# Attention with two mixture layers on one core: nine stores on ScalarE's queue, a reordered end of the first stage, and a later start of one attention pair

## The chip, the core and the metric

The kernel runs on one core of a Trainium2 chip. The metric is the device time in microseconds (us) of one execution; of several runs the median is taken. Engines are called TensorE (PE in the rows, its weight loads PEld), VectorE (DVE), ScalarE (ACT), GpSimd (POOL) and SyncE (SP, which here only issues DMAs).

## What is computed

Three layers follow one another. The first is causal window attention for 4 batches of 576 tokens and 8 heads of 64; heads 0 to 3 see the last 32 positions, heads 4 to 7 every fourth of the last 128. Its output is the 2304x512 matrix `x` of the second layer. The third layer sums eight experts, weighted by a gate that is normalised eight times over rows and columns. The reference, cut to this:

```python
scores = np.where(masks, scale * q @ k.T, -1e9)
attn = exp(scores - max) / (sum + 1e-9)
x = (attn @ v)                       # per head, then 2304 x 512
h = max(max(x @ w1, x @ w2), x @ w3) # 512 -> 768
x = h @ w_out                        # 768 -> 512
P = exp(x @ w_gate - max); 8 times: P /= row sums; P /= column sums; P *= N/E
out = sum over e of P[:, e:e+1] * (maximum(x @ w1[e], 0) @ w2[e])
```

All is float32. The second layer's weights `wm1` reach the chip as 64-bit floats (a view as pairs of 32-bit words), and the kernel turns them into float32 itself.

## The kernel before

**Split products.** TensorE takes each float32 operand as two tiles, a rounded high part (ScalarE copies it out, the `hi` or `CAST` step) and the rest (VectorE subtracts, the `lo` step). Three matmuls (high x high, high x low, low x high: `PASS`) make one product.

**Stages.** The work after the start is a list of units (`WORK`): `b.f` is six units for batch b and slice f of the second layer's first product (`up`, matmuls on line 443), `b.out` eight units for its second product (`down`, line 653). The first units are those of batch 0; unit 36 to 41 is `0.5`, 42 to 47 `1.5`, 48 to 55 `0.out`, 56 to 61 `1.0`. After each unit's matmuls `hooks(unit)` emits side work. Attention for batches 1 to 3 is such side work: `BEGIN` gives for each batch the unit at which each of its four head pairs begins, and `STAGES` says what follows how many units later: scores, mask, maximum and exponentials (`S Ma Mb Xe Ra Rb`) in the first unit, the load of v after 6, transposes and their evacuation after 8 and 9, the second product and its two parts (`V H L`) after 11. A pair's exponentials are nine activations of 96 columns on ScalarE (line 237).

**The first stage.** Attention for batch 0 has nothing beside it that TensorE could do, so it is written out by hand, as `ORDER`, together with the conversion of the first five slices of weights. Each name is one step on one engine, the digit behind it the pair or slice; on each engine the instructions stand in the order of the names. For pair p: `Sp` scores, `Rpa` reciprocal of the sum (VectorE), `Rpb` the scaling (GpSimd), `Tpg` transpose of three tiles on TensorE (`+1` puts one extra matmul ahead), `Epg` its evacuation (`EVAC` says whether by ScalarE, A, or VectorE, V), `Vpa` the second product of half a, `Hpa` and `Lpa` the high part (ScalarE) and the rest (VectorE) of its result. For slice i the nine steps of a conversion: `c1 c3 c4 c6 c7 c9` on VectorE, `c2 c5 c8` on ScalarE; `c7` gives the float32 values in tile `raw`, `c8` and `c9` split them. `c14` and `c24` are the first two steps of group 2, of double width.

**Conversions that follow.** `load_w1` does the same for each group of two slices at once (512 KB of result), while batch 0's units run. Its 64-bit input, 1 MB, sits in one of three buffers `cx`, and the next load into a buffer waits for `c7`, the last reader. The last lines of `load_w1` and, for the two groups of the first stage, a loop behind it store `raw` to a scratch tensor `wm1f`, from which batches 1 and 2 read:

```python
        for op in ops.values():          # 394: c1 ... c9
            op()
        if g < NG:
            nc.sync.dma_start(wm1f[g], raw)          # 397, seven times
...
    for g in range(2):
        nc.sync.dma_start(wm1f[g], raws[g][0])       # 778
```

**What sets the order elsewhere.** TensorE's order is that of the program throughout. Inside `ORDER` this holds for all engines; other instructions (loads, stores, conversions of later groups) are placed between by a planner, which estimates when each is ready. Behind `ORDER` and until `1.out` the planner also orders VectorE, ScalarE, GpSimd and the DMA queues. The scores of batches 1 to 3 are line 184, batch 0's are line 190; transposes line 267, evacuations 271, `V` 284, `H` 304, `L` 308. The banks of `up` are four (`ps_g`): the first result of three is copied out by ScalarE (449), the others taken by VectorE (451).

Of the kernel before, what the change touches and what calls it, by code (L numbers as in the profile page):

```python
# [25 lines left out]

OUTER = {"0.4": (0, 1), "0.5": (2,)}

BEGIN = {1: (0, 5, 10, 16), 2: (43, 60, 67, 73), 3: (91, 98, 105, 112)}
SUMS = (86, 89, 93, 96, 100, 103, 107, 110, 114)  # L30
WEIGHTS = 78
FIRST = {118: "S", 120: "A1", 121: "A2", 122: "X0", 123: "X1", 126: "Y0", 127: "Y1"}
# [10 lines left out]


LOADS = "m0 k0 w0 k1 m2 k2 g0 k3 v0 g1 v1 v2 v3 g2"
EVAC = "AAV VVV VAV AAA".split()
ORDER = (
# [5 lines left out]
)  # L53
NT, DM = B * S, H * D
F1 = 768
# [24 lines left out]
def split(nc, hi, lo, src, sub):  # L80

    nc.scalar.copy(hi, src)  # L82
    sub.tensor_tensor(out=lo, in0=src, in1=hi.bitcast(F32), op=ALU.subtract)  # L83
# [16 lines left out]
def attention_moe(ctx: ExitStack, tc: tile.TileContext, q, k, v, mask, wm1, wg, wm2, out):  # L100
    nc = tc.nc
# [220 lines left out]
    wm1f = dram.tile([NG, P, 2, 512], F32, name="wm1f")  # L322
# [7 lines left out]
    def narrow_ops(dst, bits, parts):  # L330

        low, high = (bits.rearrange("p (n w) -> p n w", w=2)[:, :, i] for i in range(2))
        z, mf = dst.bitcast(U32), high.bitcast(F32)

        def hi():
            for w, x in parts:
                nc.scalar.copy(w[:, 0], x)

        def lo():
            for w, x in parts:  # L340
                nc.vector.tensor_tensor(out=w[:, 1], in0=x, in1=w[:, 0].bitcast(F32), op=ALU.subtract)

        return {
            "c1": lambda: nc.vector.tensor_scalar(
                out=z, in0=high, scalar1=0x7FF00000, scalar2=None, op0=ALU.bitwise_and
            ),
            "c2": lambda: nc.scalar.activation(out=z, in_=z, func=AF.Relu, scale=8.0, bias=ebias),
            "c3": lambda: nc.vector.scalar_tensor_tensor(
                out=z, in0=high, scalar=0x80000000, in1=z, op0=ALU.bitwise_and, op1=ALU.bitwise_or
            ),  # L350
            "c4": lambda: nc.vector.tensor_scalar(
                out=high, in0=high, scalar1=0xFFFFF, scalar2=None, op0=ALU.bitwise_and
            ),
            "c5": lambda: nc.scalar.activation(out=mf, in_=high, func=AF.Copy, scale=2.0 ** -20, bias=1.0),
            "c6": lambda: nc.vector.scalar_tensor_tensor(
                out=mf, in0=low, scalar=2.0 ** -52, in1=mf, op0=ALU.mult, op1=ALU.add
            ),
            "c7": lambda: nc.vector.tensor_tensor(out=dst, in0=dst, in1=mf, op=ALU.mult),
            "c8": hi,
            "c9": lo,  # L360
        }

    def fetch_w1(b, g):
        raw = raw_p.tile([P, 2, 512], F32, name="raw")
        if b:
            nc.sync.dma_start(raw, wm1f[g])
            return raw, None
        t = cx_p.tile([P, KT * S], U32, name="cx", tag="cx")
        nc.sync.dma_start(t[:, 0:2048].rearrange("p (i n) -> p i n", i=2), wm1[g].bitcast(U32))
        return raw, t  # L370

    def w1_tile(g):
        if g < NG:
            return wa_p.tile([P, 2, 512], F32R, name="wa")
        return wb1_p.tile([P, 2, 512], F32R, name="wb1")
# [3 lines left out]
    def load_w1(b, g):  # L379
        begin = begun.pop(g, None)  # L380
        raw, t = fetch_w1(b, g) if begin is None else (begin[0], None)
        ws = [w1_tile(g) for _ in range(2)]
        if b:
            for i in range(2):
                split(nc, ws[i][:, 0], ws[i][:, 1], raw[:, i], nc.gpsimd)
                keep_w1(2 * g + i, ws[i])
            return ws
        if begin is None:
            parts = []
            ops = narrow_ops(raw.rearrange("p i n -> p (i n)"), t[:, 0:2048], parts)  # L390
        else:
            _, parts, ops = begin
        parts.extend((ws[i], raw[:, i]) for i in range(2))
        for op in ops.values():
            op()
        if g < NG:
            nc.sync.dma_start(wm1f[g], raw)
        return ws

    wsp = dram.tile([3 * NF1, P, 2, 512], F32, name="wsp")  # L400
# [1 line left out]
    def keep_w1(j, t):  # L402
        c = j // 3 % 2 * 256
        nc.sync.dma_start(wsp[j, :, :, c:512], t[:, :, c:512].bitcast(F32))
# [6 lines left out]
    def fetch(b, f):  # L411

        if b == 1 and f >= NF1 - 2:
            return kept.pop(f)
        if b == 2:
            return made[b][3 * f:3 * f + 3]
        ahead = 3 if b == 0 and f == NF1 - 2 else 0
        while len(made[b]) < 3 * f + 3 + ahead:
            made[b] += load_w1(b, len(made[b]) // 2)
        ws = made[b][3 * f:3 * f + 3]  # L420
        if b == 0 and f >= NF1 - 2:
            kept[f] = ws
        return ws
# [305 lines left out]
    qk, vs, raws = {}, {}, {}  # L729
# [16 lines left out]
    for p in range(H // 2):  # L746
        for name, op in attn_ops(0, p, pools[p], *qk[p], vs[p], EVAC[p]).items():
            if name not in "W X0 X1 X2 X3 X4 Ma Mb Xe".split():
# [4 lines left out]
    raw, t = raws[2]  # L753
# [4 lines left out]
    for i in range(4):  # L758
        raw, t = raws[i // 2]
# [15 lines left out]
    xtb_p = tc.alloc_tile_pool(name="xtb", bufs=1, reuse_waits="tile")  # L775
    spaces.append(xtb_p.tile([P, SPACE], F32R, name="xt"))
    for g in range(2):
        nc.sync.dma_start(wm1f[g], raws[g][0])

# [112 lines left out]
    def early(what):  # L892

        if what == "X":
            first_x.extend(fetch_x(0, nc.sync))
            return
        i = what[-1]
        if what[0] in "dT":
            (b11, b21), (b12, b22) = ((x[:, 0:2], x[:, 2:4]) for x in first_x)
            o, x, y = {"1": (b11, b12, b11), "3": (b12, b22, b12), "2": (b22, b22, b11), "4": (b21, b21, b22)}[i]  # L900
            if what[0] == "d":
                nc.vector.tensor_tensor(out=o, in0=x, in1=y, op=ALU.subtract)
            else:
                split_x(x_ops[0], what, {what: o}, nc.vector)
        elif what[0] == "w":
            ahead_w[int(i)] = fetch_w2(0, int(i))
        elif what[0] == "s":
            sums_2[int(i)] = sums_w2(ahead_w[int(i)])
        else:
            what, i = what.split(".")  # L910
            split_w2(int(i), what, ahead_w[int(i)], sums_2.get(int(i)))
# [12 lines left out]
    def hooks(unit):  # L924
# [30 lines left out]
        for what in EARLY.get(unit, "").split():  # L955
            early(what)
        for b, begin in BEGIN.items():
            for p in range(H // 2):
# [9 lines left out]
    for what, unit in zip(WORK, starts):  # L968
        b, f = what.split(".")
        b = int(b)  # L970
        if what == "3.0":
            at_p.release()
            xs_p = tc.alloc_tile_pool(name="xs", bufs=1, side="right", reuse_waits="tile")
            sm_p = tc.alloc_tile_pool(name="sm2", bufs=1, side="right", reuse_waits="tile")
        if what == "1.out":
            ordered.enter_context(tc.manual_schedule(engines={mybir.EngineType.Activation, mybir.EngineType.DVE}))
        if f == "out":
            down(b, unit)
            if b == B - 1:
                ordered.close()  # L980
        elif b == 3:
            if f == "0":
                for g, group in enumerate(groups):
                    if group[0][0] == b:
                        unit = up_quads(g, unit)
        else:
            up(b, int(f), unit)
            for g in OUTER.get(what, ()):
                wo += load_w1(0, NG + g)
# [106 lines left out]
    for i, (blk, e, n) in enumerate(stages):  # L1096
        wo, xo = w_ops.pop(i), x_ops[blk]
        raws = ahead_w.pop(i)
# [452 lines left out]
```

## Time and profile before

| what | us |
|---|---|
| median of 3 runs | 1901.3 |
| lowest and highest run | 1893.08 and 1903.84 |
| the profiled execution, its own time | 1899.56 |
| span of that execution's instructions | 1897.7 |

The rows below come from the profiled execution. In a timeline row the first number is the start in us from the span's start, the second the length; consecutive instructions of one kind are merged (`x10`), and the bracket gives the idle time of the engine just before and what ended it. PEclk is TensorE's granted clock as a share of full speed (2.4 GHz; 0.5 is 1.2 GHz).

### The profile page before, as it was taken

Reading aid. Unit: us, or ns where it says so; the run is one execution under the profiler, and the core shown is the slowest. Engines: PE = TensorE matmul, PEld = TensorE weight load, DVE = VectorE, ACT = ScalarE, POOL = GpSimd, SP = SyncE. Lnnn points to the kernel's source line nnn. Section 1 sums busy time; section 2 is a strip of 40 time slices with the busy share of each in tenths; the row PEclk is TensorE's granted clock in tenths of the full one; section 3 lists DMA queues with packets and bytes.
Section 4 is the critical chain, followed back from the end, with each engine's and each line's share of the span. In section 5 each row is a group of like instructions: output and inputs, shape, how many; then the busy total and the mean of one; then the engine's idle time right before and its main releaser. Section 6 shows DMA issues by size and latency. Waiting matters only on the chain.

```text
span 1897.7 us, 34135 instructions
## 1 busy us (share of the span) xinstructions
PE 1855.6 (98%) x12055; PEld 1745.5 (92%) x12055; DVE 1332.1 (70%) x2531; ACT 978.6 (52%) x2395; POOL 647.3 (34%) x552
## 2 busy tenths in 40 slices
PE   8899999999999999999999999999999999999998
PEld 7799999998899987999999999999989999999997
DVE  6993374677866666566687777877767677776777
ACT  6763445444554444444456555565545555555554
POOL 1123243335666667766512121121211211211111
PEclk8999999999999999999999999999999999999999
DMA  8776486866667778776977767777798676676763
GB/s 266 266 244 221 145 273 205 298 225 232 239 250 254 259 251 299 257 254 249 369 243 246 236 218 225 230 239 238 238 323 261 215 235 222 224 257 212 236 217 100
DMA packets 218441, 458.82 MB, mean 242 GB/s; under 512 B 19936, under 2 KB 102944, under 8 KB 216736
## 3 DMA queue, kind: packets, MB, share of 16 engines
q1 hardware_dynamic: 216640, 454.29, 70.9%
q10 hardware_dynamic: 1632, 2.36, 0.3%
q8 instruction: 96, 1.57, 0.3%
q14 instruction: 73, 0.60, 0.1%
HBM read 325.42 MB, written 130.81 MB: 240 GB/s over the span
## 4 chain that ended last, share of the span: by engine, by line
PE 82%; DVE 9%; DMA 5%; ACT 2%; issue 2%; POOL 1%; SPq 0%; DVEq 0%; ACTq 0%; POOLq 0%
PE po L1320 25%; PE po L1415 12%; PE po L1065 10%; PE q L1415 6%; PE p L1415 6%; PE ps L443 6%; PE q L1111 4%; PE p L1111 4%; PE ps L653 4%; DMA raw<-in_wm 1%; PE ps L573 1%; DMA vt<-in_v 1%; PE q L573 1%; DVE ts L838 1%; DVE h L1163 1%
## 5 line engine op out<-in xcount | busy, mean ns | idle before, releaser
L1320 PE MATMUL po<-wt,hop 128*128 128x256 f32 (+1 forms) x3264 | 482.9, 310 | 3.4 <-DMA wt<-wtd 3.4
L1320 PEld LDWEIGHTS po<-wt,hop 128*128 128x128 f32 x3264 | 444.8, 191 | 39.1 <-ACT wt L82 3.6
L83 POOL TENSOR_TENSOR wt<-raw,wt 128x256 fp32r<-128x256 f32 x192 | 186.2, 994 | 758.6 <-ACT wt L82 757.2
L83 DVE TENSOR_TENSOR hop<-r,hop 128x384 fp32r<-128x384 f32 x384 | 208.6, 573 | 188.5 <-ACT hop L82 188.5
L1065 PE MATMUL po<-wb,h 128*128 128x512 f32 x1152 | 295.4, 392 | 1.1 <-POOL wb L83 1.1
L1065 PEld LDWEIGHTS po<-wb,h 128*128 128x128 f32 x1152 | 213.4, 188 | 35.3 <-POOL wb L83 2.3
L82 ACT CAST hop<-r 128x384 fp32r<-128x384 f32 x384 | 188.7, 516 | 56.2 <-DVE r L1296 30.5
L443 PE MATMUL ps<-xt,wa 128*128 128x288 f32 x1296 | 187.9, 301 | 4.9 <-DVE xt L308 2.9
L443 PEld LDWEIGHTS ps<-xt,wa 128*128 128x128 f32 x1296 | 176.8, 191 | 8.7 <-DVE xt L308 3.4
L83 POOL TENSOR_TENSOR wa<-raw,wa 128x256 fp32r<-128x256 f32 (+1 forms) x107 | 131.0, 1228 | 112.9 <-ACT wa L82 103.5
L1429 ACT ACTIVATE r<-r 128x384 f32<-128x384 f32 x192 | 99.8, 525 | 128.9 <-DVE r L1428 127.9
L1415 PE MATMUL po<-xB,wa 128*128 128x384 f32 x576 | 116.9, 338 | 0.0
L1415 PE MATMUL po<-xt,wa 128*128 128x384 f32 x576 | 116.9, 338 | 0.0
L83 POOL TENSOR_TENSOR tw<-ts,tw 128x512 fp32r<-128x512 f32 x64 | 85.3, 1356 | 92.3 <-DVE h L1163 57.5
L1349 DVE SCALAR_TENSOR_TENSOR acc<-po,prob,acc 128x256 f32<-128x256 f32 x222 | 95.1, 475 | 22.3 <-PE po L1320 17.6
L83 POOL TENSOR_TENSOR wa<-sums,wa 128x512 fp32r<-128x512 f32 x64 | 89.0, 1409 | 53.8 <-ACT wa L82 30.0
L83 POOL TENSOR_TENSOR wb<-raw,wb 128x512 fp32r<-128x512 f32 x64 | 92.9, 1451 | 28.8 <-ACT wb L82 28.4
L1415 PEld LDWEIGHTS po<-xB,wa 128*128 128x128 f32 x576 | 102.5, 188 | 0.0
L1415 PEld LDWEIGHTS po<-xt,wa 128*128 128x128 f32 x576 | 102.5, 188 | 0.0
L1290 DVE TENSOR_TENSOR r<-r,r 128x384 f32<-128x384 f32 x128 | 93.1, 728 | 2.2
L799 DVE TENSOR_TENSOR sums<-raw 128x256 f32<-128x256 f32 x64 | 40.2, 628 | 73.9 <-DMA raw<-in_wm 70.0
L1331 ACT COPY mm<-po 128x256 f32<-128x256 f32 x144 | 49.6, 375 | 79.6 <-PE po L1320 79.6
(246 smaller groups left out, 3359.1 us busy)
## 6 DMA issues: line engine op xcount, KB each, us to landing
wa<-wsd SPq DMA_DIRECT2D x192, 512.0 KB, 4.5
wt<-wtd SPq DMA_DIRECT2D x256, 256.0 KB, 3.7
wsd<-wa SPq DMA_DIRECT2D x96, 512.0 KB, 3.4
raw<-in_wm SPq DMA_DIRECT2D x64, 512.0 KB, 4.3
wtd<-tw SPq DMA_DIRECT2D x128, 256.0 KB, 2.8
raw<-in_wm SPq DMA_DIRECT2D x128, 256.0 KB, 5.3
wa<-wsd SPq DMA_DIRECT2D x64, 256.0 KB, 4.7
cx<-in_wm SPq DMA_DIRECT2D x12, 1024.0 KB, 8.9
```

What stands on the lines that cost most here:

```text
L82: nc.scalar.copy(hi, src)
L83: sub.tensor_tensor(out=lo, in0=src, in1=hi.bitcast(F32), op=ALU.subtract)
L443: nc.tensor.matmul(ps, w[:, wi, kk], xt[:, xi, kk, n0:n0 + HB], start=(n == 0), stop=(n == 3 * KT - 1),)
L653: nc.tensor.matmul(ps, wo[f][:, wi, d2 * P:(d2 + 1) * P], hs[f][:, hi, a * HB:(a + 1) * HB], start=(f == 0 and n == 0), stop=(f == NF1 - 1 ...
L1065: nc.tensor.matmul(po, self.hs[f, j][:, hi, t * P:(t + 1) * P], self.ws[f][:, wi], start=(n + f + k == 0), stop=(n == NPAIR - 1 and f == 1 ...
L1111: nc.tensor.matmul(ps, wo[w][:, wi, kk], xo[x][:, xi, kk], start=(first and k == 0), stop=True if k == 5 else False, skip_group_check=not ...
L1290: nc.vector.tensor_tensor(out=r[o, n], in0=r[x, n], in1=r[y, n], op=op)
L1320: nc.tensor.matmul(self.ps[side, t][:, 0:x.shape[-1]], h[:, hi, t * P:(t + 1) * P], x, start=(first and i == 0), stop=(n == NPAIR - 1 and ...
L1331: nc.scalar.copy(m, self.ps[ORD[k][0], t][:, 0:256])
L1349: nc.vector.scalar_tensor_tensor(out=a, in0=src, scalar=g, in1=a, op0=ALU.mult, op1=ALU.add)
L1415: nc.tensor.matmul(ps[k][side], wo[k][w][:, wi, kk], xo[x][:, xi, kk], start=(first and c == 0), stop=c == 5, skip_group_check=not first,)
L1429: nc.scalar.activation(out=r, in_=r, func=AF.Relu)
```

## The change

Three things. The nine stores of `raw` to `wm1f` are issued from ScalarE's queue in place of SyncE's. The end of `ORDER` is rewritten, and pair 2's transposes are all evacuated by ScalarE, where two of three were VectorE's. Batch 2's first pair begins at unit 47 in place of 43, and all its later steps move by four units with it.

```diff
-BEGIN = {1: (0, 5, 10, 16), 2: (43, 60, 67, 73), 3: (91, 98, 105, 112)}
+BEGIN = {1: (0, 5, 10, 16), 2: (47, 60, 67, 73), 3: (91, 98, 105, 112)}
...
-EVAC = "AAV VVV VAV AAA".split()
+EVAC = "AAV VVV AAA AAA".split()
 ORDER = (
...
-    "c71 R3a R3b c22 L01 L00 T20 E20 T21 E21 T22 E22 c80 H11 c81 H10 V21 V20 c90 c32 c42 L11 L10 c91 "
-    "T30+1 E30 T31 E31 T32 E32 c52 H21 H20 c62 L21 c72 L20 V31 V30 H31 c13 c82 H30 c23 L31 c92 c33 c43 "
-    "L30 c53 c14 c24 c63 c73 c83 c93"
+    "c71 R3a R3b c22 T20 E20 T21 E21 L01 L00 T22 E22 c32 c42 c80 H11 c81 H10 V21 V20 c90 c52 L11 L10 c91 "
+    "c13 c23 T30+1 E30 T31 E31 c62 c72 T32 E32 H21 H20 c33 c43 L21 L20 c82 V31 V30 H31 H30 c53 c92 c14 "
+    "L31 L30 c24 c63 c73 c83 c93"
 )
...
         if g < NG:
-            nc.sync.dma_start(wm1f[g], raw)
+            nc.scalar.dma_start(wm1f[g], raw)
...
     for g in range(2):
-        nc.sync.dma_start(wm1f[g], raws[g][0])
+        nc.scalar.dma_start(wm1f[g], raws[g][0])
```

## Rows read from the trace of the kernel before

**Rows 1.** The page: busy time of each engine, share, instructions.

```profile
PE 1855.6 (98%) x12055; PEld 1745.5 (92%) x12055; DVE 1332.1 (70%) x2531; ACT 978.6 (52%) x2395; POOL 647.3 (34%) x552
```

**Rows 2.** Stretches of 15 us: length, busy per engine, granted clock, DMA share, GB/s.

```profile
30.00:45.00 15.00, 12.67 (x135) 10.27 (x134) 11.55 (x28) 8.66 (x23) 0.82 (x1) 0.61 0.73 244
45.00:60.00 15.00, 13.13 (x111) 12.10 (x111) 15.00 (x21) 11.19 (x31) 0.00 (x0) 0.91 0.68 226
...
105.00:120.00 15.00, 14.02 (x131) 13.32 (x131) 15.00 (x29) 9.65 (x23) 1.18 (x1) 1.00 0.76 248
```

**Rows 3.** Timeline of TensorE, end of the first stage and first units.

```profile
27.63 1.52 PE L267 MATMUL pst<-ident,sm 128*96 128x128 f32 x6
...
31.23 1.97 PE L284 MATMUL ps<-pt,vt 96*64 96x64 f32 x32 [0.23 <-DVE pt L271]
...
33.67 2.29 PE L267 MATMUL pst<-ident,sm 128*96 128x128 f32 x9
...
38.43 2.74 PE L443 MATMUL ps<-xt,wa 128*128 128x288 f32 x10
43.12 0.53 PE L443 MATMUL ps<-xt,wa 128*128 128x288 f32 x2 [1.95 <-DVE xt L308]
...
44.62 8.05 PE L443 MATMUL ps<-xt,wa 128*128 128x288 f32 x48
53.22 1.84 PE L443 MATMUL ps<-xt,wa 128*128 128x288 f32 x12 [0.55 <-DVE tmp L451]
```

**Rows 4.** Timeline of ScalarE, end of the first stage.

```profile
29.18 0.47 ACT L271 COPY pt<-pst 96x384 f32<-96x384 f32 x1 [0.69 <-PE pst L267]
...
34.56 0.47 ACT L271 COPY pt<-pst 96x384 f32<-96x384 f32 x1 [3.27 <-PE pst L267]
...
36.37 0.67 ACT L354 ACTIVATE cx<-cx 128x512 f32<-128x512 uint32 x1
36.94 1.68 ACT L304 CAST xt<-ps 128x112 fp32r<-128x112 f32 x7
```

**Rows 5.** Timeline of VectorE, the same stretch and the first units.

```profile
30.63 0.55 DVE L271 COPY pt<-pst 96x384 f32<-96x384 f32 x1 [0.45 <-PE pst L267]
...
37.07 0.69 DVE L355 SCALAR_TENSOR_TENSOR cx<-cx 128x512 f32<-128x512 uint32 x1 [2.90 <-ACT cx L354]
...
42.24 0.83 DVE L308 TENSOR_TENSOR xt<-ps,xt 128x144 fp32r<-128x144 f32 x3
...
52.71 0.45 DVE L451 TENSOR_TENSOR tmp<-ps,tmp 128x288 f32<-128x288 f32 x1
```

**Rows 6.** What SyncE's queue waited for, first 130 us: total, times, longest.

```profile
SPq L397 <- DVE raw L358: 19.3, 5, 8.0
SPq L778 <- DVE raw L358: 15.4, 1, 15.4
```

**Rows 7.** Timeline of SyncE's queue around the second store.

```profile
45.62 0.33 SPq L778 DMA_DIRECT2D wm1f<-raw  x1
46.00 1.02 SPq L369 DMA_DIRECT2D cx<-in_wm  x1
```

**Rows 8.** Tile xB: issues on ScalarE's queue, ns min/median/max, first and last start.

```profile
L888 ACTq DMA_DIRECT2D xB<-x2s x6: 366/366/477, 354.6 to 363.5; - x6
```

**Rows 9.** Timeline of TensorE, later units.

```profile
70.14 1.04 PE L184 MATMUL pss<-kt,qt 64*64 64x96 f32 x36 [1.90 <-DMA qt<-in_q]
71.11 2.73 PE L443 MATMUL ps<-xt,wa 128*128 128x288 f32 x12
...
141.12 6.60 PE L443 MATMUL ps<-xt,wa 128*128 128x288 f32 x48
149.03 9.01 PE L653 MATMUL ps<-h,wb 128*128 128x288 f32 x66 [1.31 <-ACT tmp L449]
```

**Rows 10.** Timeline of ScalarE around unit 47.

```profile
145.07 0.38 ACT L237 ACTIVATE sm<-sm,st 128x96 f32<-128x96 f32 x1 [3.48 <-DVE st L232]
...
148.59 0.39 ACT L449 COPY tmp<-ps 128x288 f32<-128x288 f32 x1
```

## The prediction

> **What bounds the kernel now.** I read the page first: TensorE is busy for 1855.6 of 1897.7 us [rows 1], so all other work together can cost at most some 42 us, and a change that leaves the matmuls alone can only win back TensorE's idle time and its slow clock where it touches them. The stretches of 15 us say where that is: from 30 to 45 TensorE ran at a mean clock of 0.61, and from 45 to 120 it is busy for 13 to 14 of 15 us while VectorE is busy for 15.00 of 15 [rows 2]. So there are two regimes: the hand-written first stage, where three engines hand work to each other, and the conversions beside batch 0's units, where VectorE is the bound. Behind about 120 us TensorE runs nearly without a gap.
>
> The timeline of TensorE names the waits. After 10 matmuls of the first unit it stands for 1.95 us until 43.12, for a result of line 308, which is L30, the last remainder of pair 3 [rows 3]; that instruction runs on VectorE from 42.24 to 43.07 [rows 5]. VectorE is late because it stood idle for 2.90 us before 37.07, waiting for c52 on ScalarE [rows 5]. ScalarE did c52 at 36.37 only, behind E30 to E32, although it was idle for 3.27 us before E30 at 34.56 [rows 4]: c52 stands behind evacuations whose transposes had not run. That is one chain: a conversion step in the wrong place on ScalarE, an idle VectorE, a late L30, an idle TensorE.
>
> **Part 1, the end of the order.** On VectorE two evacuations of 0.55 us each [rows 5] go to ScalarE, and five conversion steps (c13, c62, c72, c33, c43; c62 is the row of 0.69 [rows 5], none is longer) move into the hole, because c52 now stands ahead of E30. Gone: 2.90 of idle time and 1.10 of copies, together 4.0. New idle time, an estimate from the rows: 0.3 before c90, as c80 now stands behind three evacuations of 0.47 [rows 4], and 0.7 before L21. For that: H21 started at 36.94 [rows 4], behind c52 (0.67, about 0.57 until the next instruction starts); without c52 ahead of it, and with TensorE 0.45 earlier (below), it starts near 35.9, and L21 near 36.4; the five steps end near 35.7. So VectorE is 4.0 - 1.0 = 3.0 us ahead, and L30 ends at 43.07 - 3.0 + 0.6 = 40.7, where 0.6 is the double-width c14, now ahead of L30 in place of behind it.
>
> On TensorE, E22 follows T22 on a free ScalarE at about 30.0 in place of 30.63 on VectorE [rows 5], so the 32 matmuls of 31.23 [rows 3] and all up to the first unit start some 0.45 earlier: first unit at 38.0, its eleventh matmul due 2.74 later [rows 3], at 40.7. L30 ends then, and the wait of 1.95 goes. TensorE gains 0.45 + 1.95 = 2.4 there. The clock may add to that: the 48 matmuls behind the wait take 8.05 us [rows 3], the same count at the full clock takes 6.60 [rows 9], and without the wait the clock should rise sooner; 1.45 us is the most that it can give there. But at 53.22 TensorE waits for a bank that VectorE frees at 52.71 [rows 3, 5], behind conversions, and VectorE is then full until 120 [rows 2]. So what lasts is VectorE's lead, 3.0 us, not TensorE's. Bounds: 0, if the planner, which reorders VectorE behind the first stage, puts the freeing of banks later by the same amount; 4.4, if the bank is also freed when TensorE wants it (0.45 + 1.95 + 1.45 + 0.55). I take **-3.0**, VectorE's lead, since its busy row says that it is the bound.
>
> **Part 2, the stores.** SyncE's queue stood 15.4 us before the second store and 19.3 before five later ones [rows 6], which looks like loads held up. But the next load goes into a `cx` buffer that the same c7 must release: the store issues at 45.62, the load at 46.00 [rows 7], so without the store it starts 0.4 earlier and not 15. Had the loads been held up, the only wait of TensorE for one in this region could go: 1.90 us for q, and the slow 12 matmuls behind it, 2.73 against 1.84 [rows 9, 3], together 2.8. By the Trainium skill (page "DMA: Bandwidth & Descriptors", section "Issuing engines are not separate DMA queues") issuing from several engines saves the issue time alone, as all transfers run on the same 16 DMA engines; by that the sum keeps this 2.8 out, and the row of 0.4 us agrees.
>
> On ScalarE nine issues are new, 0.37 each by the nearest row [rows 8], 3.3 us in all. ScalarE is busy for 10 to 11 of 15 us where they fall [rows 2], and a store needs the same c7 as the c8 that ScalarE runs anyway, so as written it adds no wait. Behind it stand bank copies (line 449), evacuations and activations, whose users are TensorE and VectorE. If each issue delayed the chain once, 3.3; if SyncE's shorter queue helps, -2.8. I take **+0.4**, one issue on the path, as idle time on ScalarE covers the rest; if the order put a store ahead of ready work, the cover is gone (second rival).
>
> **Part 3, the later pair.** At the end of unit 47 TensorE waits 1.31 us for a bank until 149.03 [rows 9]. ScalarE frees it with the copy of 148.59, and before it ran a pair's nine exponentials from 145.07 on [rows 10], those of batch 2's first pair, begun at unit 43. Begun at unit 47 they run beside `0.out`, whose results VectorE takes away, so no copy is behind them. Moved with them: scores on TensorE (36 small matmuls, the same count), mask and maximum on VectorE, the scaling on GpSimd, which also splits operands for the gate there, and later the load of v, transposes and `V`. The loads of q and k only need the buffers of the last pair of batch 1 and lie early. The pair still ends two units before the next begins at 60. Bounds: -1.31, the whole wait; +0.5, if GpSimd's scaling delays a gate operand. I take **-1.3**.
>
> **Sum.** -3.0 + 0.4 - 1.3 = -3.9. The profiled execution took 1899.6, which is 1.7 below the median of 1901.3; against the median, 1901.3 - 3.9 = 1897.4, and I predict **1897.4 us**. That is 0.2%. About 0.5% (9.5 us) is what a measurement of this kernel can tell from no change; the three runs alone lie 10.8 apart.
>
> **Rivals.** *More goes* (0.15): the wait for q and its slow clock go too, because with the whole stage 3 us earlier the loads spread differently; 1897.4 - 2.8 = 1894.6, and with part 1 at its upper end 1893. To pass 9.5, all of these and another 1.3 of waits on VectorE must go: for it speaks that these waits share one cause, against it that VectorE stays full.
>
> *ScalarE is held by the stores* (0.08, the slower side): its queue runs in order, as the 3.27 us before E30 show, with c52 ready behind [rows 4]. The mechanism: the planner's estimate puts a store ahead of copies that are ready, while VectorE, which is late against the estimate, has not finished c7. SyncE stood up to 8.0 us for one store [rows 6]. TensorE has four banks, a unit takes 1.84 [rows 3], so a hold longer than some 4 us reaches it. Three holds of 8.0 less 4 each are 12; 1897.4 + 12 = 1909 or, with the clock lost in each wait (0.9 as at 71.11 [rows 9]), 1912. It decides if a store stands ahead of line 449 or 271 with c7 late by over 4 us. The Trainium skill ("TensorE: Matmul & The Clock Gate", section "Architectural detail: the array is 16× 32×32, not 1× 128×128") calls ScalarE's queue strictly first in, first out; that is in line with the row of 3.27, and speaks against the stores' new place.
>
> *VectorE's lead is lost again* (0.15): the planner gives another order behind the first stage, banks are freed as late as before, and the changes of part 1 and 2 cancel; only part 3 stays, 1901.3 - 1.3 = 1900, or nothing, 1901.
>
> **How the numbers follow.** The forecast (0.62) has its own range from 1894 to 1900: part 1 down to -4.4 and up to -1.5, part 3 up to -0.5, the stores up to 1.5. With "more goes" and "lead lost" the range is **1890 to 1902**; it leaves out the held ScalarE and the rare case that nearly every wait goes. Faster by over 0.5% needs the far end of "more goes", or a lucky median: 0.15. Slower: 0.08. Within: 0.77.
>
> **What would show it.** Right: no idle of VectorE near 37, L30 done near 41, no wait of about 2 us in the first unit, E30's idle before it much shorter, the bank at 53.22 near 50, the wait at 149.03 gone, and the point where `0.out` starts some 4 us earlier. Wrong: TensorE reaches unit 20 as late as before (lead lost), ScalarE stands at a DMA issue (held), or the time falls by more than 9.5 us, which is more than the waits named here hold and would mean that something outside these three parts moved.

## Result, and the profile of the changed kernel

| | before | changed |
|---|---|---|
| median of 13 runs each, us | 1899.93 | 1908.62 |
| the profiled execution, its own time | 1899.56 | 1905.21 |
| span of its instructions | 1897.7 | 1903.3 |

The ratio is 1.0052, with a 95% interval from 1.0037 to 1.0066: slower by 0.5%, some 10 us by the ratio and 8.7 between the medians, where 3.9 us less were predicted. The time lies outside the range. The profiled execution of the changed kernel is 3.4 us below its own median, so the two traces differ by 5.65 us only.

The page shows no new work. This is its row of busy times, which answers to [rows 1]:

```profile
PE 1856.1 (98%) x12055; PEld 1749.1 (92%) x12055; DVE 1334.0 (70%) x2529; ACT 980.8 (52%) x2397; POOL 647.7 (34%) x552
```

Two instructions have gone from VectorE to ScalarE. TensorE's weight loads are busy for 3.6 us longer, no other row by more than 2.2, and the matmuls by 0.5. So the loss is waiting. The stretches of 15 us, which answer to [rows 2], say where:

```profile
60.00:75.00 15.00, 12.09 (x107) 11.06 (x106) 14.87 (x26) 9.13 (x31) 2.71 (x2) 0.79 0.74 263
75.00:90.00 15.00, 10.38 (x86) 10.00 (x86) 15.00 (x22) 12.27 (x34) 2.95 (x2) 0.78 0.57 189
...
105.00:120.00 15.00, 10.39 (x72) 9.91 (x69) 15.00 (x27) 11.94 (x36) 2.40 (x1) 0.80 0.63 248
```

From 105 to 120 us TensorE is busy for 10.39 us at a mean clock of 0.80, where it had 14.02 at 1.00 [rows 2]. From 75 to 90 it has 10.38 at 0.78; before, that stretch was

```profile
75.00:90.00 15.00, 13.35 (x168) 12.47 (x166) 14.85 (x21) 10.87 (x35) 3.71 (x2) 0.99 0.74 261
```

`0.out` starts at 157.73 in place of 149.03, 8.7 us later, with the scores of batch 2's first pair now just ahead of it in place of four units earlier. From there to the end of the span it takes 1745.6 us, 1748.7 before, so the whole loss lies ahead of `0.out`. Of the 8.7 us, 1.6 lie ahead of the end of c71 (30.29 in place of 28.71), up to which `ORDER` is unchanged. From there to the end of L30 the changed kernel is 0.5 faster, and from L30 to `0.out` it takes 113.6 us in place of 106.0: 7.7 more. The timeline of TensorE names the waits, in answer to [rows 3, 9]:

```profile
36.84 0.88 PE L267 MATMUL pst<-ident,sm 128*96 128x128 f32 x3 [1.74 <-ACT pt L271]
...
44.17 0.54 PE L443 MATMUL ps<-xt,wa 128*128 128x288 f32 x2 [1.44 <-DVE xt L308]
...
63.16 4.55 PE L443 MATMUL ps<-xt,wa 128*128 128x288 f32 x22 [2.67 <-DVE wa L341]
...
84.25 1.49 PE L267 MATMUL pst<-ident,sm 128*96 128x128 f32 x6 [4.62 <-DVE xt L308]
85.39 3.23 PE L443 MATMUL ps<-xt,wa 128*128 128x288 f32 x12
...
98.82 1.85 PE L443 MATMUL ps<-xt,wa 128*128 128x288 f32 x12
...
115.03 1.52 PE L267 MATMUL pst<-ident,sm 128*96 128x128 f32 x6 [4.03 <-POOL sm L256]
116.19 3.23 PE L443 MATMUL ps<-xt,wa 128*128 128x288 f32 x12
...
157.73 2.51 PE L653 MATMUL ps<-h,wb 128*128 128x288 f32 x17
```

Two waits of over 4 us are new, both for steps of batch 1's attention: the remainder of its first pair (line 308), which empties the bank that the next transposes write, and the scaled probabilities of its fourth (line 256). Behind each, the granted clock is 0.50 and 12 matmuls take 3.23 us in place of 1.85. Two smaller ones are for converted weights, 2.31 us at 59.64 and 2.67 at 63.16. The wait of 1.31 us ahead of `0.out` and that of 1.90 for q [rows 9] are gone.

Why is line 308 late at 84? VectorE, a little before:

```profile
80.22 1.21 DVE L348 SCALAR_TENSOR_TENSOR raw<-cx,raw 128x1024 uint32<-128x1024 uint32 x1
81.35 1.21 DVE L355 SCALAR_TENSOR_TENSOR cx<-cx 128x1024 f32<-128x1024 uint32 x1
82.49 1.21 DVE L348 SCALAR_TENSOR_TENSOR raw<-cx,raw 128x1024 uint32<-128x1024 uint32 x1
83.62 0.81 DVE L308 TENSOR_TENSOR xt<-pso,xt 128x320 fp32r<-128x320 f32 x2
```

and ScalarE in the same stretch, where the first half of the same step (line 304) stands behind two conversions:

```profile
76.67 1.16 ACT L354 ACTIVATE cx<-cx 128x1024 f32<-128x1024 uint32 x1
78.09 1.15 ACT L347 ACTIVATE raw<-raw,ebias 128x1024 uint32<-128x1024 uint32 x1 [0.26 <-ACT cx L354]
79.15 0.68 ACT L304 CAST xt<-pso 128x320 fp32r<-128x320 f32 x2
```

VectorE does not stand still, ScalarE for 0.26 us only. They convert weights of groups 5 to 7 while TensorE needs the attention step behind them. At 103 us VectorE does stand, at the first step of group 9, for its 1 MB load; behind it comes the row maximum (line 232) of the fourth pair, without which ScalarE can't begin the exponentials, VectorE the reciprocal (253), or GpSimd the scaling (256):

```profile
103.75 0.69 DVE L344 TENSOR_SCALAR raw<-cx 128x1024 uint32<-128x1024 uint32 x1 [2.15 <-DMA cx<-in_wm]
104.36 0.69 DVE L341 TENSOR_TENSOR wa<-raw,wa 128x512 fp32r<-128x512 f32 x1
104.96 1.05 DVE L232 TENSOR_REDUCE st<-sm 128x9 f32<-128x864 f32 x1
...
112.19 0.21 DVE L253 RECIPROCAL st<-st 128x9 f32<-128x9 f32 x1
```

In the kernel before, the same two steps stand the other way round, VectorE waits for no load, and TensorE does not wait for the fourth pair's scaling:

```profile
97.44 1.04 DVE L232 TENSOR_REDUCE st<-sm 128x9 f32<-128x864 f32 x1
98.40 0.68 DVE L344 TENSOR_SCALAR raw<-cx 128x1024 uint32<-128x1024 uint32 x1
```

So the first theory: the change gave the planner another order on VectorE and ScalarE behind the first stage, and in it conversions stand ahead of attention results that TensorE waits for. Its rivals: ScalarE is held by the nine issues; or the rewritten `ORDER` itself is worse; or VectorE is full, so that no order of it would help.

### The profile page after: what moved, and what is told of

It is laid out like the page before. It is cut to its first block, busy times and chain, and to the rows that moved or that the text cites. A ratio compares the mean times of both kernels' runs of the same rounds, so it can differ in the third digit from the quotient of the medians.

```text
span 1903.3 us, 34133 instructions
## 1 busy us (share of the span) xinstructions
PE 1856.1 (98%) x12055; PEld 1749.1 (92%) x12055; DVE 1334.0 (70%) x2529; ACT 980.8 (52%) x2397; POOL 647.7 (34%) x552
## 4 chain that ended last, share of the span: by engine, by line
PE 83%; DVE 7%; DMA 3%; ACT 2%; issue 1%; POOL 1%; DVEq 0%; ACTq 0%; SPq 0%; POOLq 0%
PE po L1320 25%; PE po L1415 12%; PE po L1065 10%; PE ps L443 7%; PE p L1415 6%; PE q L1415 6%; PE q L1111 4%; PE p L1111 4%; PE ps L653 3%; DMA raw<-in_wm 1%; PE ps L573 1%; PE q L573 1%; DVE h L1163 1%; DVE ts L838 1%; DVE sums L799 1%
```

## Experiments

Each ratio is to the kernel before, on the same chip, with its 95% interval; medians of 6 to 12 runs. The kernel before had a median of 1898.52 us beside the four runs of the first group, 1899.24 beside the next four and 1900.22 beside the last four.

### One part alone, and the change without its stores

Stores alone, the kernel before with:

```diff
-            nc.sync.dma_start(wm1f[g], raw)
+            nc.scalar.dma_start(wm1f[g], raw)
...
-        nc.sync.dma_start(wm1f[g], raws[g][0])
+        nc.scalar.dma_start(wm1f[g], raws[g][0])
```

> Only the nine stores are issued from ScalarE's queue; the first stage's order and the later pair are as before. Theory S (the stores cost): the loss of the changed kernel, 8.7 us in the medians, is theirs, since with them the planner puts VectorE and ScalarE in another order behind the first stage; here 6 to 9 us slower than before, with waits of 2 us or more for line 341, 337 or 308 on TensorE between 55 and 120 us. Theory O (the rewritten end of the order costs): here within 1.5 us of before, and the longest wait of TensorE in that stretch stays at 2 us or less.

1901.49 us, 1.0013 (1.0000 to 1.0027).

Order alone, the kernel before with the new `EVAC`, and `ORDER` as in the change:

```diff
-EVAC = "AAV VVV VAV AAA".split()
+EVAC = "AAV VVV AAA AAA".split()
```

> Only the end of the first stage's order and the evacuations are changed. Theory O: 6 to 9 us slower than before, the waits of 2 us or more between 55 and 120 us are here. Theory S: 0 to 3 us faster than before, as the lead of VectorE was forecast to give 3.0. In both, TensorE should wait near 1.7 us for an evacuation of pair 3, since c23 stands ahead of E30 on ScalarE and waits for c13, and the end of L30 should come 0.5 to 1 us earlier against c71 than before.

1899.94 us, 1.0001 (0.9986 to 1.0017). Two things expected of its trace did not come: L30 ended 16.2 us after c71, later and not earlier, and TensorE's wait for pair 3's evacuation was 0.28 us.

The later beginning alone:

```diff
-BEGIN = {1: (0, 5, 10, 16), 2: (43, 60, 67, 73), 3: (91, 98, 105, 112)}
+BEGIN = {1: (0, 5, 10, 16), 2: (47, 60, 67, 73), 3: (91, 98, 105, 112)}
```

> Only batch 2's first pair begins at unit 47. All theories: 1.3 us faster than before, the wait of 1.31 us at the start of 0.out gone, nothing else moved; up to 120 us the trace is that of before.

1899.23 us, 0.9995 (0.9980 to 1.0011), and the wait of 1.31 us ahead of `0.out` is gone here too.

The whole change without the stores' move:

```diff
-            nc.scalar.dma_start(wm1f[g], raw)
+            nc.sync.dma_start(wm1f[g], raw)
...
-        nc.scalar.dma_start(wm1f[g], raws[g][0])
+        nc.sync.dma_start(wm1f[g], raws[g][0])
```

> The changed kernel with the stores back on SyncE's queue: new order and later pair. Theory S: 1 to 4 us faster than before. Theory O: 5 to 8 us slower than before, as the changed kernel. If the loss needs both (theory B: each alone is harmless, together the loads of 1 MB come too late), 1 to 4 us faster here too, but then stores_only is within 1.5 us of before.

1898.91 us, 1.0000 (0.9984 to 1.0015).

None of the parts costs 10 us: the three alone add up to 0.9 thousandths, the whole is 5.2. And order with the later beginning brings nothing, where 4.3 us had been forecast for them. Its trace shows L30 late:

```profile
39.95 0.69 DVE L308 TENSOR_TENSOR xt<-ps,xt 128x112 fp32r<-128x112 f32 x2
...
44.56 0.69 DVE L344 TENSOR_SCALAR raw<-cx 128x1024 uint32<-128x1024 uint32 x1 [3.92 <-DMA cx<-in_wm]
45.17 0.85 DVE L308 TENSOR_TENSOR xt<-ps,xt 128x144 fp32r<-128x144 f32 x3
```

The planner put the first step of group 3 between the pieces of L30. Its load is 1 MB and not there yet; VectorE stands for 3.92 us, and TensorE waits 4.53 us for L30.

Three runs have the `ORDER` of before: the stores alone, the later beginning alone, and the change without the new order (below). Their traces show that the hole of 2.90 us, from which the forecast was worked out, was smaller in other executions. From the end of c71 to the first unit TensorE's granted clock was 0.50 (1.2 GHz) in the trace of the kernel before, where TensorE had just waited 1.21 us for v, and 1.00 in all three. The row of each, and VectorE at c62 in the run of the stores alone (compare [rows 5]):

```profile
28.71:38.43 9.72, 8.77 (x89) 6.60 (x88) 6.30 (x16) 5.49 (x16) 1.63 (x1) 0.50 1.01 320
...
31.45:38.85 7.40, 4.96 (x86) 3.84 (x86) 6.31 (x17) 5.03 (x16) 1.63 (x1) 1.00 1.03 315
...
37.53 0.69 DVE L355 SCALAR_TENSOR_TENSOR cx<-cx 128x512 f32<-128x512 uint32 x1 [1.02 <-ACT cx L354]
```

VectorE's hole is 1.02, 1.02 and 1.03 us in the three, and L30 ends 12.0 to 12.1 us after c71, where it took 14.36 in the trace of the kernel before.

### Two parts at a time, and a third queue

The change without the later beginning:

```diff
-BEGIN = {1: (0, 5, 10, 16), 2: (47, 60, 67, 73), 3: (91, 98, 105, 112)}
+BEGIN = {1: (0, 5, 10, 16), 2: (43, 60, 67, 73), 3: (91, 98, 105, 112)}
```

> The change without its third part (group begun at unit 43 again): stores on ScalarE's queue and the new order. Alone the stores gave 1.0013 and the order 1.0001. Theory 1 (stores and order together give the planner another order of conversions and another time for the 1 MB loads): about 1.004 to 1.005, 8 to 10 us over the kernel before, with TensorE's waits for L308 and L256 of 4 us and more again. Rival (the effects of the parts add up, and the loss needs the later beginning): 1.001 to 1.002, 2 to 4 us.

1906.20 us, 1.0042 (1.0028 to 1.0056).

The change without the new order (`EVAC` and `ORDER` of before):

```diff
-EVAC = "AAV VVV AAA AAA".split()
+EVAC = "AAV VVV VAV AAA".split()
```

> The change without its first part: stores on ScalarE's queue and the group begun at unit 47, the order of before. Theory 1 (the loss comes of stores and new order together): about what the stores alone gave, 1.000 to 1.002. Rival (the later beginning makes the stores dear, as conversions crowd): 1.004 to 1.005, 8 to 10 us.

1900.63 us, 1.0012 (0.9999 to 1.0025).

The whole change, with the stores issued by GpSimd:

```diff
-            nc.scalar.dma_start(wm1f[g], raw)
+            nc.gpsimd.dma_start(wm1f[g], raw)
...
-        nc.scalar.dma_start(wm1f[g], raws[g][0])
+        nc.gpsimd.dma_start(wm1f[g], raws[g][0])
```

> The whole change, but the nine stores are issued by GpSimd's queue; VectorE's order is that of the changed kernel but for one pair of steps, ScalarE's is the same without the nine issues, SyncE's the same. Theory 1 (the loss is in the order and in the times of the loads on SyncE's queue): still 1.004 to 1.006, 8 to 11 us over the kernel before. Rival (ScalarE is held by the nine issues and by what they wait for): back to 1.000, as without the stores' move, since ScalarE holds none.

1909.53 us, 1.0058 (1.0039 to 1.0077).

The loss needs the stores' move and the new order together; what the later beginning adds (1.0052 against 1.0042, 1.0012 against 1.0013) can't be told from nothing. And it is not that ScalarE is held by the nine issues: with none of them on it the kernel is as slow as the change. What the two have in common is the order: up to 160 us VectorE's differs between their traces by one swapped pair of steps, ScalarE's not at all. The waits are the same two:

```profile
85.70 1.49 PE L267 MATMUL pst<-ident,sm 128*96 128x128 f32 x6 [3.75 <-DVE xt L308]
116.02 1.52 PE L267 MATMUL pst<-ident,sm 128*96 128x128 f32 x6 [4.48 <-POOL sm L256]
```

In the changed kernel's own trace the issues take 0.33 to 0.36 us each, and ScalarE goes on beside them, as here (`ACTq` is its DMA issue):

```profile
72.20 0.37 ACT L237 ACTIVATE sm<-sm,st 128x96 f32<-128x96 f32 x1
72.23 0.33 ACTq L397 DMA_DIRECT2D wm1f<-raw  x1
72.46 0.19 ACT L237 ACTIVATION_READ_ACCUMULATOR sm<-sm,st 128x1 f32 x1
```

### The lead given back

Order and later beginning, stores on SyncE, with the first step of group 3 kept behind L30 on VectorE (an order of issue, no wait):

```diff
-        for op in ops.values():
-            op()
+        for name, op in ops.items():
+            if g == 3 and name == "c1":
+                with tc.issue_after(held[0]):
+                    op()
+            else:
+                op()
...
+            if name == "L30":
+                held.append(next(i for i in reversed(nc.cur_bb.bb.instructions) if i.engine == mybir.EngineType.DVE))
```

> New order and later beginning, stores on SyncE's queue, and the first conversion of group 3 on VectorE kept behind L30. Without that pin this ratio was 1.0000, and that conversion stood 3.92 us for its 1 MB load ahead of L30. Theory (this stand is where the lead that was forecast for VectorE went): L30 ends 3 to 4 us earlier against c71, TensorE's wait for L308 near 46 falls from 4.53 to under 1, and the kernel is 2 to 4 us faster, 0.998 to 0.999. Rival (the lead is worth nothing as the next units wait for wa and for other conversions anyway): the wait is short and the time is the same, 1.000.

1900.71 us, 1.0009 (0.9996 to 1.0021). Counted from the end of c71, L30 ends after 12.2 us, where it took 16.8 without the pin, 14.36 in the trace of the kernel before, and 12.0 to 12.1 in the three at the full clock. So the stand at the load is gone and the time is no lower (1.0009 against 1.0000 without the pin); but L30 is no earlier than the old order has it at the full clock. Nor does the run show what an early L30 is worth by itself, since the planner answered the pin with another order: up to 160 us at least 48 of VectorE's 226 steps stand elsewhere than without it. `0.out` starts at 152.16, and on the way TensorE waits for the fourth pair again:

```profile
109.57 1.52 PE L267 MATMUL pst<-ident,sm 128*96 128x128 f32 x6 [3.68 <-POOL sm L256]
110.74 3.23 PE L447 MATMUL ps<-xt,wa 128*128 128x288 f32 x12
```

and on VectorE a first conversion step stands at its load, ahead of that pair's reciprocal:

```profile
106.89 0.69 DVE L344 TENSOR_SCALAR raw<-cx 128x1024 uint32<-128x1024 uint32 x1 [2.10 <-DMA cx<-in_wm]
107.50 0.21 DVE L253 RECIPROCAL st<-st 128x9 f32<-128x9 f32 x1
```

### The order put right by pins

The changed kernel, all three parts kept, with conversion steps pinned behind attention steps by the same means. The names are step and group on the left, batch, pair and step on the right.

First, the conversions that stood ahead of the first pair's L and H:

```diff
+    BEHIND = {"c36": "b10L1", "c66": "b10L1", "c37": "b10L1", "c65": "b10L1",
+              "c55": "b10H1", "c56": "b10H1", "c27": "b10H1"}
...
+        with tc.issue_after(last[BEHIND[name]]) if name in BEHIND else ExitStack():
+            op()
```

> The changed kernel, with the conversion steps of groups 5 to 7 that stood ahead of the second batch's first L (L308) on VectorE and its H (L304) on ScalarE pinned behind them. In the changed kernel TensorE waited 4.62 us for that L308 at 84.25 and then ran 12 matmuls at half clock (3.23 instead of 1.85). Theory (planned order: conversions put ahead of attention results that TensorE waits for): the wait falls to under 1.5 us, the time to 4 to 6 us under the changed kernel, a ratio to the kernel before of 1.002 to 1.003. Rival (VectorE is full there, so what is put first only makes something else late): the wait goes elsewhere and the ratio stays at 1.004 to 1.006.

1905.83 us, 1.0035 (1.0022 to 1.0048), between what the theory and its rival gave. The wait at the first pair falls, the other one stays:

```profile
82.70 0.83 PE L267 MATMUL pst<-ident,sm 128*96 128x128 f32 x6 [1.29 <-DVE xt L308]
...
114.15 1.51 PE L267 MATMUL pst<-ident,sm 128*96 128x128 f32 x6 [4.64 <-POOL sm L256]
```

Second, the first steps of groups 9 and 10 behind the fourth pair:

```diff
+    BEHIND = {"c19": "b13Ra", "c110": "b13Ra", "c29": "b13Xe", "c210": "b13Xe"}
```

> The changed kernel, with the first conversion step of groups 9 and 10 pinned behind the reciprocal of the second batch's fourth pair (L253) on VectorE, and their second step behind its exponentials (L237) on ScalarE. In the changed kernel VectorE stood 2.15 us at that first step for the 1 MB load, with the row maximum (L232) behind it, and TensorE waited 4.03 us for L256 at 115.03. Theory (planned order): that wait falls to under 1 us and the time by 4 to 6 us, a ratio to the kernel before of 1.002 to 1.003. Rival (VectorE is full there): ratio stays at 1.004 to 1.006.

1904.81 us, 1.0027 (1.0017 to 1.0036). Here it is the other way round:

```profile
86.47 1.49 PE L267 MATMUL pst<-ident,sm 128*96 128x128 f32 x6 [4.61 <-DVE xt L308]
...
112.83 0.50 PE L267 MATMUL pst<-ident,sm 128*96 128x128 f32 x3 [1.49 <-DVE xt L308]
114.13 0.50 PE L267 MATMUL pst<-ident,sm 128*96 128x128 f32 x3 [0.80 <-DVE xt L308]
```

Both sets together, the two lists in one `BEHIND`:

> The changed kernel with both sets of pins, stores still on ScalarE's queue, the new order and the later beginning. Theory (planned order): both waits of over 4 us are gone with the slow clock behind them, and the time comes down by 8 to 10 us to that of the kernel before, a ratio of 0.999 to 1.001. Rival (the waits only move, since VectorE has as much to do as before): a ratio of 1.004 or more.

1902.68 us, 1.0009 (0.9997 to 1.0021). The first set takes 1.7 thousandths from 5.2, the second 2.5, both 4.3: they add up, within their intervals, and what is left is within 0.21% of the kernel before. So eleven pins, which change nothing but the order of issue, take back some four fifths of the loss, by the central values. They act on more than eleven steps, as the planner moves others with them: up to 160 us at least 14 of VectorE's 221 steps with the first set and 31 with both stand elsewhere than in the changed kernel's trace. One wait did move on, as its rival had it: TensorE still stands for 3.05 us at 112.66, now for a remainder of the third pair, which on VectorE is behind the first step of group 10 and its load:

```profile
110.69 0.69 DVE L344 TENSOR_SCALAR raw<-cx 128x1024 uint32<-128x1024 uint32 x1 [2.76 <-DMA cx<-in_wm]
...
111.66 1.43 DVE L308 TENSOR_TENSOR xt<-pso,xt 128x144 fp32r<-128x144 f32 x5
```

In this trace VectorE stands at three loads, 2.81, 2.70 and 2.76 us, 8.3 us in all, more than in the changed kernel (0.63, 1.10 and 2.15). The first of them makes TensorE wait 4.05 us for L30, in place of 1.44. The time is lower all the same.

Last, the pins without the stores' move, and group 3 behind L30:

```diff
+    BEHIND = {"c13": "b030L",
...
-            nc.scalar.dma_start(wm1f[g], raw)
+            nc.sync.dma_start(wm1f[g], raw)
```

> New order and later beginning, stores on SyncE's queue, with these pins and the pin that keeps the first step of group 3 behind L30. With that last pin alone the ratio was 1.0009: L30 ended 12.2 us after the seventh-step conversion c71 instead of 14.4, but TensorE then waited 2.19 us for queries, 3.91 for ScalarE's copy of a transpose and 3.68 for L256. Theory (the lead is real but spent at the later attention results that stand behind conversions): the waits near 80 and 110 us go and the time is 3 to 6 us under the kernel before, 0.997 to 0.9985. Rival (a wait of another sort takes their place, VectorE being full from 45 to 120 us): 0.9995 to 1.001.

1898.13 us, 0.9997 (0.9985 to 1.0010): as fast as the kernel before, no faster. TensorE has no wait of over 1.5 us from 72 to 160 in its trace, but four before that (3.09 and 2.39 for ScalarE's evacuations, 1.99 for q, 1.96 for wa). No version that was run beats the kernel before by more than its interval.

## Why the prediction was wrong

**Where the bound lies.** The regime from 45 to 120 us was read as "VectorE is the bound", from its 15.00 of 15 [rows 2], and so VectorE's lead was taken for TensorE's gain. (By stretch it is 14.85 to 15.00, and TensorE has 12.45 to 14.02, not 13 to 14.) This step failed: VectorE was full, but partly with conversions that nobody needed yet. The pins show it. They put conversion steps behind attention steps and take none away, VectorE then stood 8.3 us at loads where it had stood 3.9, and the kernel was faster. What sets the time there is when TensorE gets each attention result and each weight, so the order within the full engine, not its load. What a lead on one step is worth by itself, no run isolates.

**Part 1, -3.0.** Measured alone 1.0001, +0.2 us with an interval from -2.7 to +3.2. The chain of c52, an idle VectorE and a late L30 was read rightly from its rows, but its largest term was mis-sized: the hole of 2.90 us [rows 5] belongs to one execution whose first stage ran at a clock of 0.50, and at 1.00 it is 1.02 or 1.03. With 1.0 in its place the part's own sum gives 2.1 - 1.0, a lead of 1.1 in place of 3.0, and none of it is seen: at a clock of 0.97 the new order, with group 3 held back, ends L30 12.2 us after c71 (the last run above), the old one at 1.00 after 12.0 to 12.1. Without that pin it ends later still, since the planner placed group 3's first step ahead of L30's last pieces, at a load that had not landed (3.92 us, 2.07 in the run of the order alone, 0.63 in the changed kernel, where L30 ends after 13.8). New too was a wait of ScalarE that the working of new idle time left out: c23 stands ahead of E30, and ScalarE stood 1.58 us at it for VectorE's c13, so TensorE waited 1.74 at 36.84. ScalarE of the changed kernel, c23 and then E30 and E31:

```profile
35.70 0.72 ACT L347 ACTIVATE raw<-raw,ebias 128x512 uint32<-128x512 uint32 x1 [1.58 <-DVE raw L344]
36.33 0.83 ACT L271 COPY pt<-pst 96x384 f32<-96x384 f32 x2
```

**Part 2, +0.4.** Measured alone 1.0013, about +2.5 us, which lies within its bounds. What the move does in the whole change was none of the effects priced. The nine issues cost ScalarE about what [rows 8] gave and no run shows that they delayed anything; earlier loads did not come of it, as forecast: alone the move won nothing. By the Trainium skill ("DMA: Bandwidth & Descriptors", "Issuing engines are not separate DMA queues") the gain of another issuing engine is the issue time alone; the ratios of 1.0013, 1.0052 and 1.0058 with ScalarE and GpSimd agree in that none shows a gain. What was priced at nothing is that the move changes the planner's order.

**The sum.** Parts 1 and 2 were added as if each acted by itself. Together with the order the stores cost 4.2 thousandths, some 8 us, where they cost 1.3 and 0.1 alone. The step that put the time outside the range is the upper bound of part 1, "0, if the planner [...] puts the freeing of banks later by the same amount": a reordering has no floor at nothing. It was thought of as losing a lead, and priced so in the rival *VectorE's lead is lost again* (1900 or 1901). In fact it put conversions ahead of two steps that TensorE waits for, at 4.62 and 4.03 us with 1.4 of slow clock behind each (3.23 against 1.85). That is 11.4 us, and not all of it is loss: TensorE waited 1.31 us at the first of these places before, and in the runs of the later beginning alone, the order alone and the change without the stores' move, none of them slower, 2.80 to 3.14 at the first, with the slow clock behind it in two of them, and up to 1.61 at the second. The pins took back 8.2 us. Apart from that, the forecast's own range does not follow from the terms named for it: -4.4 + 0.4 - 1.3 gives 1896 at its lower end, not 1894, and -1.5 - 0.5 + 1.5 gives 1901.

**Part 3, -1.3.** The wait of 1.31 us is gone in every kernel with the later beginning and the pair's exponentials run beside `0.out`, as said. Its worth, 0.9995 alone (from -3.8 to +2.1 us), can't be told from nothing or from -1.3.

**The rivals.** *ScalarE is held by the stores* named 1909 to 1912, close to what came (the profiled execution took 1905.21, the median is 1908.62), for a reason that the GpSimd run excludes. That the number came close is luck. *VectorE's lead is lost again* named the planner's other order, but let it cost no more than the lead. *More goes* did not happen: the wait for q went, and others came.

What stays open: why the planner, without the stores in SyncE's queue, puts those conversions earlier. That it does is seen in the order of the instructions and does not depend on which other queue takes the stores. That it then expects the 1 MB loads sooner, as their queue is shorter, is only argued. For it speaks that behind 46 us VectorE never stood at such a load in the kernel before or in the three without the stores' move and without pins, and two or three times in each of the five with it. Which pairs of steps the planner swaps, and so whether a given move costs 0 or 8 us, could not be told ahead of the trace.

## What to carry to other kernels

Where a planner orders part of a kernel, moving one DMA to another queue is a change of order on every engine: compare the order of the instructions and look for what now stands ahead of the results that the bounding engine waits for, before costing the issue itself. An engine that is busy all the time is not thereby the bound; if part of its work runs ahead of need, the place of a few steps in its queue can be worth microseconds while its idle time costs nothing. Before a hole in one trace is priced, look at the granted clock beside it: here it was 2.90 us at 0.50 and 1.02 at 1.00. Pins that keep a handful of prefetching steps behind results that are due can take such a loss back without undoing the change.

## What the runs showed of the hardware

Some of VectorE's steps took over 1 us longer while GpSimd's scaling ran, which the working of part 1 did not count. In the changed kernel the step of 0.68 us took 1.73 beside it:

```profile
31.21 1.73 DVE L348 SCALAR_TENSOR_TENSOR raw<-cx,raw 128x512 uint32<-128x512 uint32 x1
...
36.91 0.68 DVE L348 SCALAR_TENSOR_TENSOR raw<-cx,raw 128x512 uint32<-128x512 uint32 x1
```

with GpSimd at work from 30.76 to 32.39:

```profile
30.76 1.63 POOL L256 TENSOR_TENSOR sm<-sm,st 128x864 f32<-128x864 f32 x1 [4.00 <-DVE st L253]
...
112.57 2.40 POOL L256 TENSOR_TENSOR sm<-sm,st 128x864 f32<-128x864 f32 x1 [22.29 <-ACT raw L347]
```

The same step at double width took 2.29 in place of 1.21 at 113.77, beside the scaling of 112.57, and the scaling itself took 2.40 in place of 1.63 there. The first step ended 0.55 us after the scaling, which is about its own length alone, as if it had stood until then. The Trainium skill ("SBUF — State Buffer", "SBUF: two separate sides") says that a VectorE operation with two inputs in SBUF and one of GpSimd lock each other out of a shared port for a whole instruction; these rows agree.

Not every wait costs TensorE its clock. Behind the 4.62 and 4.03 us the next 12 matmuls took 3.23; behind the 1.28 us that was left of the first with both sets of pins they took 1.84 (below). The length of the wait alone does not tell: at the same place the granted clock stayed at 1.00 behind 3.10 us in the kernel without the stores' move, and was 0.50 behind 2.80 us in that with the later beginning alone, where the 12 matmuls took 3.23.

```profile
82.80 0.83 PE L267 MATMUL pst<-ident,sm 128*96 128x128 f32 x6 [1.28 <-DVE xt L308]
83.39 1.84 PE L449 MATMUL ps<-xt,wa 128*128 128x288 f32 x12
```
